# A new order list for a fused attention and token-mixing kernel, planned with other costs for the turned tiles of u

## Chip, cores and metric

The kernel runs on one core of one Trainium2 chip. The metric is the device time of one execution in microseconds (us), as the median of several runs; lower is better.

## What is computed

Two layers follow each other. The first is attention with 8 heads of 64 over 768 tokens, for 4 batches, where a token sees the 96 tokens up to itself and the first 8 tokens of all, with a bias that falls with the distance. The second takes its output as x (4 x 768 x 512) and mixes tokens and channels:

```
scores = q @ k.T / 8 + bias            # kept: 96 local columns and the 8 global ones
x      = softmax(scores) @ v           # heads side by side: 512 channels
theta  = x @ w_theta
y      = w_tok_r @ (x * cos(theta)) + w_tok_i @ (x * sin(theta))
u      = x + y
out    = u + relu(u @ w_ch)
```

## The kernel before

Tokens lie in 6 tiles of 128 (`NT`), heads in 4 pairs (`NP`). Each batch b goes through four stages, which are written down as about a thousand steps: `attention(b, p)` for each pair of heads, `theta(b)` for each tile of tokens, `mixing(b)` and `channel(b)`.

- `attention` turns q and k (on TensorE, L555, or for later batches on VectorE, L560, into `kq`), copies some keys aside (`kS`, L572 and L573), makes scores (TensorE, L611), exponents (ScalarE, L619), weighs them with the bias (VectorE, L628 and L633), multiplies with v (L678; some rows of v are copied to `vs` first, L439 and L443) and divides by the sums (VectorE, L698 and L699, into `x`). x is then turned on TensorE (L720) and copied to `xT` (L723).
- `theta` multiplies xT with w_theta (L796), takes cosine and sine on ScalarE (L804 and L807, into `cs`) and makes `zri` = x times both on VectorE (L813).
- `mixing` runs over two halves of the tokens and four chunks of channels. Each of these 8 sums takes 12 matmuls of 384 columns (L838), in groups of 4 that each wait for two tiles of `zri`, and ends with the addition of xT on VectorE (L847, into `uT`).
- `channel` multiplies uT with w_ch (L874), for each of 6 tiles of tokens, and needs u in its natural layout (`un`) for the last sum. In batches 0 and 3 TensorE turns it (L870). In batches 1 and 2 (`u_far`) the tile is turned by `turn_far`, described next. In these batches ScalarE makes the relu (L906) and GpSimd the sum (L909); elsewhere VectorE does both (L900). The result is stored from SyncE's queue (L917).

`turn_far` takes a tile out to DRAM and back. VectorE turns squares of 32 x 32 into one of two buffers (`squares_turn`, L756, shown as `w_nat<-uT` in the profile, since the buffers lie in `w_nat`'s place). SyncE issues four DMAs, one for each quarter of the partitions, that write the squares to DRAM at their turned places (`out_there`, L760, `far_u<-w_nat`), and then one that reads the tile back (`back`, L765, `un<-far_u`). As there are two buffers, the L756 of a tile waits until the DMAs of the tile two before have landed.

No loop fixes the order in which the engines get these steps. A planner (`Plan.order`) simulates the engines with a cost for each step and a delay (`HOP`) between a step and one on another engine that needs it, picks steps by priority, and issues them in the order of its planned starts. Two tables, keyed by the number of a step, move it: `plan.shifts` adds to its priority, `plan.only` fixes its engine where several could do it. On the chip each engine then works through its own queue in that order and waits wherever a semaphore is not there yet, so an instruction that waits holds up all that stands behind it in its queue. A step's cost has no effect on the chip but through this order. The steps of `turn_far` are, in the planner:

```
s1 = add("DVE", 0.12 + n * T / 960.0, squares_turn, ready + log[-2:-1] + s_wT[1], prio)
i1 = add("SP", 4 * 0.45, out_there, [s1], prio)
h1 = add("HW", 0.22 * n, lambda: None, [i1], 0)
log.append(h1)
i2 = add("SP", 0.45, back, [h1] + free, prio)
return add("HW", 0.1 * n, lambda: None, [i2], 0)
```

Here n is 4 for a tile of u, HW is a pretended engine for the time of the transfers, and `HOP["HW"]` is the delay after it.

Loads come from GpSimd's queue (`load`, with L392 and L477 for q and k, L397 for v); the 36 k and 36 q loads of L477 each fetch a block of 32 columns. GpSimd also does its share of the copies and the twelve sums L909, in the same queue.

Of the kernel before, what the change touches and what calls it, by code (L numbers as in the profile page):

```python
# [48 lines left out]
        self.end = None  # L49


HOP = {"PE": 0.28, "ACT": 0.18, "DVE": 0.18, "POOL": 0.25, "SP": 0.0, "DMA": 1.6, "STORE": 1.5, "LAND": 0.0, "HW": 2.0}

# [10 lines left out]
class Plan:  # L66
# [12 lines left out]
    def add(self, *a, **k):  # L79
        s = Step(*a, **k)  # L80
        self.steps.append(s)
        return s
# [141 lines left out]
def kernel(  # L224
# [15 lines left out]
    T = 128  # L240
    NT = S // T
    DM = H * D
    NP = H // 2
# [16 lines left out]
    def wide(bank):  # L260
        return PS[bank.got]

    def narrow(bank):
# [19 lines left out]
    x_t = [sb.tile([T, NP, NT, T], BF, name=f"x_{i}") for i in range(2)]  # L283
    xT = [sb.tile([T, NP, NT, T], BF, name=f"xT_{i}") for i in range(2)]
# [17 lines left out]
    r_t = [spare[:, (2 + 2 * i) * DM:(4 + 2 * i) * DM].bitcast(FP) for i in range(2)]  # L302
    plan = Plan(N_WIDE, N_NARROW)
    plan.shifts = {
        111: -90, 121: -459, 127: -298, 132: -268, 139: -9, 141: -38, 163: 504, 175: -9, 183: -174, 184: -602,
        194: 118, 196: 173, 199: -116, 204: -309, 205: -290, 208: 715, 215: 265, 219: 866, 221: 499, 223: 142,
        226: -289, 228: 607, 229: -721, 231: 76, 237: 504, 239: 1014, 244: 40, 247: -27, 248: -23, 251: -275,
        252: 324, 255: 54, 260: -47, 262: -53, 263: 789, 267: 222, 271: 1188, 275: 1795, 287: 280, 297: -209,
        298: 384, 304: 101, 305: 151, 310: -165, 312: -26, 336: -182, 372: 626, 391: -244, 408: -608, 412: 250,
        424: -45, 425: -223, 428: -44, 438: 124, 440: -117, 441: 1504, 444: 411, 448: 813, 452: -183, 457: -142,  # L310
        459: 5, 467: -339, 492: -90, 507: 231, 532: 229, 573: 345, 603: -266, 613: 117, 616: -5, 629: -91,
        632: -223, 635: 421, 638: -81, 647: -434, 649: 607, 653: 325, 655: -397, 656: -123, 665: -99, 668: 610,
        674: -2583, 675: 104, 677: -1014, 678: -634, 680: 199, 683: 347, 684: 205, 694: -193, 695: -59, 696: -155,
        698: -817, 704: 82, 708: 415, 714: 1451, 720: -238, 722: -196, 724: -915, 726: 411, 735: 115, 740: -165,
        765: 22, 851: 366, 880: -74, 893: 450, 900: -148, 903: -381, 904: 234, 910: 1872, 921: 605, 928: 2328,
        929: 2961, 946: -125, 950: 695, 952: -307, 956: -727, 980: 148, 994: 166, 1004: 1458, 1014: -220, 1015: -59,
        1020: 41, 1021: 512, 1028: -146, 1034: 53, 1035: 1834, 1043: 104, 1044: 100,
    }
    plan.only = {
        38: "POOL", 45: "POOL", 64: "POOL", 67: "POOL", 77: "POOL", 112: "DVE", 149: "DVE", 176: "POOL", 191: "ACT",  # L320
        194: "ACT", 228: "ACT", 244: "DVE", 281: "DVE", 287: "ACT", 299: "ACT", 318: "POOL", 333: "ACT", 337: "POOL",
        389: "ACT", 553: "DVE", 613: "DVE", 616: "DVE", 649: "DVE", 810: "POOL", 831: "DVE", 852: "DVE", 894: "POOL",
        951: "ACT",
    }
    add = plan.add
    ANY = list(range(N_WIDE + N_NARROW - 1, -1, -1))
# [209 lines left out]
    th_log, cs_log, o_log, mix_log, ch_log = {}, [], [], {}, {}  # L536

    def attention(b, p):
        pr = 1000 * b + 100 * p
        n = b * NP + p  # L540
# [4 lines left out]
        old = att_log.get(n - 3, [[], None])  # L545
# [38 lines left out]
        for g, (c0, n_c) in enumerate(groups):  # L584
# [50 lines left out]
            if by_pe:  # L635
                need.append(add("PE", 0.107 * n_c, far_off, [tk if (b, p) not in by_dve else None, old[1], s_dist, s_I[h0], s_I[h0 + 1]], pr + 18 + g,
                                takes=sc, dense=True, ins=4))
            s1 = add("PE", 0.0535 * n_c * cold, scores, need, pr + 20 + g, takes=None if by_pe else sc, tiled=1,
                     ins=8 if g == 0 else 16)
# [46 lines left out]
        for t0, t1 in ([(0, 2), (2, 4), (4, 6)] if fine else [(0, NT)]):  # L686
            nt = t1 - t0
            away = (b, p) in x_far
            mine = po[t0 // 2:t0 // 2 + 1] if fine else po

            def norm(t0=t0, t1=t1, nt=nt, mine=mine):
                dst = x_t[b % 2][:, p, t0:t1, :].rearrange("p t (h d) -> p h t d", h=2)
                if len(mine) == 1:
                    if fine:
                        ps = narrow(mine[0])[:, 0:2 * nt * (D + 1)].rearrange("p (h t d) -> p h t d", h=2, t=nt)
                    else:
                        ps = wide(mine[0])[:, :, 0:NT * (D + 1)].rearrange("p h (t d) -> p h t d", t=NT)
                    nc.vector.reciprocal(rc[:, :, t0:t1], ps[:, :, :, D])  # L698
                    nc.vector.tensor_mul(dst, ps[:, :, :, 0:D],  # L699
                                         rc[:, :, t0:t1, None].to_broadcast([T, 2, nt, D]))  # L700
                else:
                    for hh in range(2):
                        ps = narrow(mine[hh])[:, 0:NT * (D + 1)].rearrange("p (t d) -> p t d", t=NT)
                        nc.vector.reciprocal(rc[:, hh, :], ps[:, :, D])
                        nc.vector.tensor_mul(dst[:, hh, :, :], ps[:, :, 0:D],
                                             rc[:, hh, :, None].to_broadcast([T, NT, D]))
            nm = add("DVE", 0.55 if fine else 0.85 + 0.3 * len(po), norm,
                     [value_steps[t0 // 2] if fine else last] + [z_done[b - 2, st] for st in range(NT) if b >= 2],
                     pr + 60 + t0, frees=mine)
            if away:  # L710
                cx = turn_far(f"x{b}{p}", NT, x_t[b % 2][:, p, :, :], xT[b % 2][:, p, :, :], [nm], mix_log.get(b - 2, []), pr + 70)
                for t in range(t0, t1):
                    xT_done[b, p, t] = cx
                continue
            bk = Bank(False, ANY)

            def turn_x(t0=t0, t1=t1, bk=bk):
                ps = narrow(bk).bitcast(BF)
                for t in range(t0, t1):
                    nc.tensor.transpose(ps[:, (t - t0) * T:(t - t0 + 1) * T], x_t[b % 2][:, p, t, :], ident)  # L720

            def copy_x(copy, t0=t0, t1=t1, nt=nt, bk=bk):
                copy(out=xT[b % 2][:, p, t0:t1, :].rearrange("p t c -> p (t c)"),  # L723
                     in_=narrow(bk).bitcast(BF)[:, 0:nt * T])
            tx = add("PE", 0.0567 * nt, turn_x, [nm], pr + 70 + t0, takes=bk, ins=2 * nt)
            cx = any_of(copy_x, [tx] + mix_log.get(b - 2, []), pr + 71 + t0,
                        {"DVE": (0.08 + 0.07 * nt, 0.0), "ACT": (0.2 + 0.084 * nt, 0.0)}, frees=[bk])
            for t in range(t0, t1):
                xT_done[b, p, t] = cx
# [15 lines left out]
            got.append(any_of(cp, [t1], prio + st, {"DVE": (0.5, 0.0), "ACT": (0.72, 0.0)}, frees=[bk]))  # L745
        return got

    def turn_far(name, n, src, dst, ready, free, prio):


        log = sq_log[n]
        sq = sq_t[n][len(log) % 2]
        away = far_away.tile([n, T, T], BF, name=f"far_{name}")

        def squares_turn():
            nc.vector.transpose(out=sq[:, 0:n, :], in_=src)  # L756

        def out_there():
            for g in range(4):
                nc.sync.dma_start(  # L760
                    out=away.rearrange("n (j b) (i a) -> i b (n j) a", b=32, a=32)[g],
                    in_=sq[32 * g:32 * g + 32, 0:n, :].rearrange("b n (j a) -> b (n j) a", a=32))

        def back():
            nc.sync.dma_start(out=dst, in_=away.rearrange("n q a -> q n a"))  # L765
        s1 = add("DVE", 0.12 + n * T / 960.0, squares_turn, ready + log[-2:-1] + s_wT[1], prio)
        i1 = add("SP", 4 * 0.45, out_there, [s1], prio)
        h1 = add("HW", 0.22 * n, lambda: None, [i1], 0)
        log.append(h1)
        i2 = add("SP", 0.45, back, [h1] + free, prio)  # L770
        return add("HW", 0.1 * n, lambda: None, [i2], 0)

    sq_log = {NT: [], NP: []}
    s_wT = [None, None]
    sins = []
    by_two = ()
    z_done, u_done = {}, {}
# [77 lines left out]
    def channel(b):  # L855
        for tt in range(NT):
            pr = 1000 * (b + 1) + 500 + 10 * (NP * (tt // 3 + 1)) + 5 + tt
            late = b == B - 1 and tt >= parts[b][-1][0]
# [3 lines left out]
            o, un = o_t[n_o[0] % 4], un_t[n_o[0] % 4]  # L862
            n_o[0] += 1
            old = [o_log[-4]] if len(o_log) >= 4 else []
# [17 lines left out]
            away = (b, tt) in u_far  # L882
            if away:
                cu = turn_far(f"u{b}{tt}", NP, uT[b % 2][:, :, tt * T:(tt + 1) * T],
                              un.rearrange("p (c a) -> p c a", c=NP), u_done[b, tt], old, pr - 300)
            for c0, c1 in split:
                more = -30 * (c0 > 0)
                tu = tu if away else add("PE", 0.06 * (c1 - c0), lambda f=turn, a=c0, z=c1: f(a, z), [tu] + u_done[b, tt][c0:c1],
# [7 lines left out]
            for hf in range(halves):  # L896
# [5 lines left out]
                if (b, tt) in pool_add:  # L902
# [8 lines left out]
                    s1 = add("POOL", 1.3, add_u, [r1, cu] + old, pr - 400)  # L911
                    add_log.append(s1)
                else:
                    s1 = add("DVE", 0.1 + 0.55 / halves, f_o, [t1[hf], cu] + old, pr - 400 + hf, frees=[bks[hf]])
# [75 lines left out]
```

## Time and profile before

| what | us |
|---|---|
| median of 3 runs (172.05 to 172.56) | 172.32 |
| the profiled execution, its own time | 172.21 |
| its span, first to last instruction | 170.4 |
| TensorE busy | 156.4 (92%) |
| VectorE busy | 138.5 (81%) |
| ScalarE busy | 119.8 (70%) |
| GpSimd busy | 106.6 (63%) |
| mean granted TensorE clock | 0.996 |

The profiled execution took 1.8 us more than its span, before the first and after the last instruction. PE is TensorE, DVE VectorE, ACT ScalarE, POOL GpSimd and SP SyncE; SPq is SyncE's sequencer, which issues DMAs. A row of the timeline gives the start in the span, the length, the engine, the line of the kernel, the operation and the tiles (out<-in), and in brackets the idle time of the engine before it and what ended that.

### The profile page before, as it was taken

How to read it: one execution, taken by the hardware profiler on the slowest of the kernel's cores; microseconds unless marked ns; L12 is line 12 of the kernel's file. 1: busy time of each engine (PE TensorE's matmuls, PEld its weight loads, DVE VectorE, ACT ScalarE, POOL GpSimd, SP SyncE). 2: the span in 40 equal slices, each digit the busy share in tenths (PEclk: the TensorE clock that was granted, in tenths of full speed). 3: DMA queues.
4: the chain of work that ended last, by engine and by line, in shares of the span. 5: the costliest groups of instructions: out<-in, count | busy, mean ns of one | idle time of the engine just before them, and what ended most of it. 6: DMA issues, size and time to landing. Idle time of an engine off the chain costs nothing.

```text
span 170.4 us, 4571 instructions
## 1 busy us (share of the span) xinstructions
PE 156.4 (92%) x1817; PEld 93.7 (55%) x1830; DVE 138.5 (81%) x260; ACT 119.8 (70%) x191; POOL 106.6 (63%) x140
## 2 busy tenths in 40 slices
PE   7867888999999999999999999489999999999990
PEld 2335564665675655556666654245566655556560
DVE  4687986868999999999999989989998877432662
ACT  6996898939999399999785387867736968600130
POOL 7997931338997999999999985844800502530000
PEclk9999999999999999999999999999999999999998
DMA  4999999999999999999999999957424466730135
GB/s 108 168 157 174 204 204 205 206 172 157 53 132 121 106 219 115 91 238 125 85 106 104 125 138 118 94 164 188 143 30 72 62 155 104 196 137 0 42 141 186
DMA packets 124549, 22.78 MB, mean 134 GB/s; under 512 B 113648, under 2 KB 121584, under 8 KB 124528
## 3 DMA queue, kind: packets, MB, share of 16 engines
q0 software_dynamic: 88976, 12.66, 107.5%
q1 hardware_dynamic: 35408, 9.70, 25.4%
q8 instruction: 14, 0.23, 0.6%
q10 hardware_dynamic: 144, 0.13, 0.2%
q14 instruction: 7, 0.06, 0.1%
HBM read 27.26 MB, written 7.86 MB: 206 GB/s over the span
## 4 chain that ended last, share of the span: by engine, by line
PE 63%; DMA 14%; POOL 7%; SPq 4%; DVE 4%; ACT 4%; issue 2%; DVEq 0%; POOLq 0%
PE ps L838 29%; PE ps L874 10%; DMA zri<-in_moe_w_tok_r_dram 9%; PE ps L796 8%; DMA far_u<-w_nat 6%; PE ps L611 5%; SPq L760 4%; PE ps L678 4%; POOL v L397 3%; PE ps L720 2%; PE ps L739 2%; POOL q L392 2%; PE ps L870 2%; POOL k L392 1%; ACT ex L619 1%
## 5 line engine op out<-in xcount | busy, mean ns | idle before, releaser
L838 PE MATMUL ps<-wT,zri 128*128 128x384 bf16 x384 | 70.0, 326 | 2.6 <-DVE zri L813 2.6
L838 PEld LDWEIGHTS <-zri 128*128 128x128 bf16 x384 | 34.9, 98 | 24.9 <-DVE zri L813 3.2
L619 ACT ACTIVATE ex<-ps 128x1024 bf16<-128x1024 f32 (+1 forms) x44 | 40.6, 949 | 7.9 <-PE ps L611 7.3
L909 POOL TENSOR_TENSOR o<-w_nat,un 128x512 f32<-128x512 f32 x12 | 15.3, 1287 | 25.7 <-issue 9.3
L477 POOL DMA_DIRECT2D k<-in_k_dram x36 | 26.1, 787 | 5.6 <-DMA w_nat<-in_moe_w_tok_i_dram 1.8
L477 POOL DMA_DIRECT2D q<-in_q_dram x36 | 26.2, 797 | 3.0 <-DMA v<-in_v_dram 1.9
L847 DVE TENSOR_TENSOR uT<-xT,ps 128x384 bf16<-128x384 bf16 x32 | 17.4, 547 | 8.0 <-PE ps L838 7.6
L874 PE MATMUL ps<-w_ch,uT 128*128 128x512 bf16 (+1 forms) x93 | 22.9, 370 | 0.5
L796 PE MATMUL ps<-w_th,xT 128*128 128x512 bf16 x90 | 22.7, 379 | 0.3
L813 DVE TENSOR_TENSOR zri<-x,cs 128x1024 bf16<-128x1024 bf16 x24 | 20.1, 858 | 3.0 <-ACT cs L807 2.8
L633 DVE TENSOR_TENSOR ex<-ex,Wm 128x1024 bf16<-128x1024 bf16 x28 | 19.4, 701 | 0.1
L397 POOL DMA_DIRECT2D v<-in_v_dram x16 | 17.7, 1104 | 1.8 <-DMA w_nat<-in_moe_w_tok_i_dram 1.8
L804 ACT ACTIVATE cs<-ps,halfpi 128x512 bf16<-128x512 f32 x24 | 16.2, 694 | 2.3 <-DVE zri L813 1.1
L699 DVE TENSOR_TENSOR x<-ps,rec 128x256 bf16<-128x256 f32 (+1 forms) x26 | 16.9, 650 | 0.9
L678 PEld LDWEIGHTS <-ex 128*128 128x128 bf16 x352 | 13.9, 97 | 5.3 <-issue 1.4
L678 PE MATMUL ps<-v,ex 128*128 128x65 bf16 x224 | 15.0, 193 | 1.0 <-ACT ex L619 1.0
L611 PE MATMUL ps<-kq 64*128 64x128 bf16 (+1 forms) x192 | 14.3, 226 | 0.6 <-DVE kq L560 0.3
L807 ACT ACTIVATE cs<-ps 128x512 bf16<-128x512 f32 x24 | 14.4, 605 | 0.5 <-PE ps L796 0.5
L879 ACT COPY un<-ps 128x512 bf16<-128x512 bf16 x7 | 4.0, 590 | 14.9 <-PE ps L870 14.9
L796 PEld LDWEIGHTS <-xT 128*128 128x128 bf16 x96 | 9.1, 98 | 9.4
L874 PEld LDWEIGHTS <-uT 128*128 128x128 bf16 x100 | 9.0, 97 | 7.9 <-issue 0.4
L723 ACT COPY xT<-ps 128x768 bf16<-128x768 bf16 (+1 forms) x14 | 8.3, 590 | 7.1 <-PE ps L720 7.1
(78 smaller groups left out, 236.0 us busy)
## 6 DMA issues: line engine op xcount, KB each, us to landing
out_dram<-o SPq DMA_DIRECT2D x23, 256.0 KB, 2.8
v<-in_v_dram POOLq DMA_DIRECT2D x16, 192.0 KB, 6.0
k<-in_k_dram POOLq DMA_DIRECT2D x36, 48.0 KB, 4.7
q<-in_q_dram POOLq DMA_DIRECT2D x36, 48.0 KB, 4.5
far_u<-w_nat SPq DMA_DIRECT2D x48, 32.0 KB, 2.7
un<-far_u SPq DMA_DIRECT2D x12, 128.0 KB, 2.8
zri<-in_moe_w_tok_r_dram POOLq DMA_DIRECT2D x2, 576.0 KB, 13.0
w_nat<-in_moe_w_tok_i_dram POOLq DMA_DIRECT2D x2, 576.0 KB, 17.1
```

Of the source, the lines that this page charges most:

```text
L397: nc.gpsimd.dma_start(out=v_t[b % 2][:, h0:h0 + n, :, 0:D].rearrange("p h t d -> p (h t) d"), in_=v[b, h0:h0 + n].rearrange("h (t p) d -> ...
L477: nc.gpsimd.dma_start(out=squares(dst, b, h0).rearrange("p (j c) -> p j c", c=32)[r0:r0 + 32], in_=src[b, h0 + hh, :, 32 * dh:32 * dh + 32 ...
L611: nc.tensor.matmul(ps[hh][:, col * T:(col + w) * T], lhsT=lhsT, rhs=kq3[R, i // 3, 1, i % 3 * T:(i % 3 + w) * T], start=not by_pe, stop=no ...
L619: nc.scalar.activation(dst, wide(sc[0])[:, :, 0:n_c * T], AF.Exp, scale=scale)
L633: nc.vector.tensor_mul(dst, dst, w)
L678: nc.tensor.matmul(dst, lhsT=l, rhs=r, start=(i == 0), stop=(i == len(mms) - 1))
L699: nc.vector.tensor_mul(dst, ps[:, :, :, 0:D], rc[:, :, t0:t1, None].to_broadcast([T, 2, nt, D]))
L796: nc.tensor.matmul(tiles()[:, i, :], lhsT=xT[b % 2][:, p, st + i, :], rhs=w_th[:, p, :], start=(p == 0), stop=(p == NP - 1))
L813: nc.vector.tensor_mul(zri[b % 2][:, st, :, :].rearrange("p w (c d) -> p w c d", c=NP), x_t[b % 2][:, None, :, st, :].to_broadcast([T, 2, ...
L838: nc.tensor.matmul(narrow(bk)[:, 0:nt * T], lhsT=zri[b % 2][:, st, wi, c * T:(c + 1) * T], rhs=wT[wi][:, st, cols], start=(k + i == 0), st ...
L847: nc.vector.tensor_add(uT[b % 2][:, c, cols], xT[b % 2][:, c, n0:n0 + nt, :].rearrange("p t c -> p (t c)"), narrow(bk)[:, 0:nt * T])
L874: nc.tensor.matmul(narrow(bks[hf])[:, 0:wide_n], lhsT=uT[b % 2][:, c, tt * T:(tt + 1) * T], rhs=w_ch[:, c, hf * wide_n:(hf + 1) * wide_n], ...
```

## The change

The costs of a tile that is turned through DRAM are changed in the planner, with another number for batch 1 (2.5) than for batch 2 (0.3), and both tables are made anew for them. No computation, tile, buffer or DMA is added or removed.

```diff
-HOP = {..., "LAND": 0.0, "HW": 2.0}
+HOP = {..., "LAND": 0.0, "HW": 1.4}
...
     plan.shifts = {
-        111: -90, 121: -459, 127: -298, 132: -268, 139: -9, ...
+        26: 675, 67: 708, 97: 6, 111: -163, 127: 1472, ...
     }
     plan.only = {
-        38: "POOL", 45: "POOL", 64: "POOL", 67: "POOL", 77: "POOL", ...
+        67: "DVE", 76: "ACT", 112: "DVE", 130: "DVE", 131: "DVE", ...
     }
...
-    def turn_far(name, n, src, dst, ready, free, prio):
+    def turn_far(name, n, src, dst, ready, free, prio, late):
...
-        s1 = add("DVE", 0.12 + n * T / 960.0, squares_turn, ready + log[-2:-1] + s_wT[1], prio)
-        i1 = add("SP", 4 * 0.45, out_there, [s1], prio)
-        h1 = add("HW", 0.22 * n, lambda: None, [i1], 0)
+        s1 = add("DVE", 0.17 + n * T / 960.0, squares_turn, ready + log[-2:-1] + s_wT[1], prio)
+        i1 = add("SP", 2.0 + 0.2 * late, out_there, [s1], prio)
+        h1 = add("HW", 0.1 * n, lambda: None, [i1], 0)
         log.append(h1)
         i2 = add("SP", 0.45, back, [h1] + free, prio)
-        return add("HW", 0.1 * n, lambda: None, [i2], 0)
+        i2.ways["SP"] = (0.45, back, late)
+        h2 = add("HW", 0.1 * n, lambda: None, [i2], 0)
+        h2.ways["HW"] = (0.1 * n, h2.emit, late)
+        return h2
...
                 cu = turn_far(f"u{b}{tt}", NP, uT[b % 2][:, :, tt * T:(tt + 1) * T],
-                              un.rearrange("p (c a) -> p c a", c=NP), u_done[b, tt], old, pr - 300)
+                              un.rearrange("p (c a) -> p c a", c=NP), u_done[b, tt], old, pr - 300, 2.5 if b == 1 else 0.3)
```

The third number of an entry in `ways` is a delay before the step may start. The tables have 155 entries before and 147 after; no shift is the same in both, and 5 of the fixed engines are. In the changed file the lines of `turn_far` are one lower (L755, L759 and L764) and those of `theta` and all below it two higher (L815 for `zri`, L840 for the mixing, L911 for GpSimd's sums).

## Prediction

> **What bounds the kernel now.** First the page. TensorE is busy for 92% of the span, and its slices fall short in two places: up to 28 us, and at 106 to 119 us. GpSimd is full up to 106, mostly with loads.
>
> ```profile
> PE   7867888999999999999999999489999999999990
> POOL 7997931338997999999999985844800502530000
> ```
>
> Between the two TensorE never waits for 0.15 us at a time, so the kernel is its work plus these idle times. The order adds or removes no matmul, so what it can move is the idle time: 5.2 us up to 28 us (the bracketed waits of PE's timeline, the start included) and 2.9 us at 106 to 117. PE's timeline shows the second place:
>
> ```profile
> 105.80 1.14 PE L838 MATMUL ps<-wT,zri 128*128 128x384 bf16 x6
> 109.03 0.50 PE L838 MATMUL ps<-wT,zri 128*128 128x384 bf16 x2 [2.10 <-DVE zri L813]
> ...
> 111.41 2.77 PE L838 MATMUL ps<-wT,zri 128*128 128x384 bf16 x16 [0.52 <-DVE zri L813]
> ...
> 116.83 0.34 PE L611 MATMUL ps<-kq 64*128 64x256 bf16 x4 [0.26 <-DVE kq L560]
> ```
>
> Each of the three waits for VectorE: 2.10 + 0.52 + 0.26 = 2.88 us. VectorE's own timeline, and GpSimd's beside it:
>
> ```profile
> 102.37 0.71 DVE L756 STREAM_TRANSPOSE w_nat<-uT 128x512 bf16<-128x512 bf16 x1 [0.89 <-DMA far_u<-w_nat]
> 103.01 0.65 DVE L813 TENSOR_TENSOR zri<-x,cs 128x1024 bf16<-128x1024 bf16 x1
> 103.58 0.70 DVE L756 STREAM_TRANSPOSE w_nat<-uT 128x512 bf16<-128x512 bf16 x1
> 104.20 4.78 DVE L813 TENSOR_TENSOR zri<-x,cs 128x1024 bf16<-128x1024 bf16 x3
> ...
> 112.95 0.71 DVE L756 STREAM_TRANSPOSE w_nat<-uT 128x512 bf16<-128x512 bf16 x1 [0.42 <-DMA far_u<-w_nat]
> ```
> ```profile
> 106.14 2.28 POOL L909 TENSOR_TENSOR o<-w_nat,un 128x512 f32<-128x512 f32 x2
> 108.35 1.09 POOL L443 COPY vs<-v 32x520 bf16<-32x520 bf16 x1
> ```
>
> Two things hold VectorE up. A turn L756 waits for a way out to land (0.89 and 0.42). And three zri take 4.78, where one takes 0.65: the third stretches to 108.98 while GpSimd makes two sums. Last, the DMAs, in the window 86 to 112 and then 124 to 150, with the median from issue to landing:
>
> ```profile
> far_u<-w_nat SPq DMA_DIRECT2D x20, 32.0 KB, 5.0
> ...
> un<-far_u SPq DMA_DIRECT2D x3, 128.0 KB, 6.0
> ```
> ```profile
> far_u<-w_nat SPq DMA_DIRECT2D x24, 32.0 KB, 2.2
> un<-far_u SPq DMA_DIRECT2D x6, 128.0 KB, 2.7
> ```
>
> Batch 1's tiles leave beside GpSimd's loads, and take twice as long. The change's premise is in the trace.
>
> **What the planner now reckons.** From the end of a turn to the release of its buffer it reckoned 1.8 + 0.88 + 2.0 = 4.7 us; now, for batch 1, 2.5 + 0.4 + 1.4 = 4.3. From there to the tile's return it reckoned 0.45 + 0.4 + 2.0 = 2.9; now 2.5 + 0.45 + 2.5 + 0.4 + 1.4 = 7.3. So the way back is longer, as the trace asks, but what VectorE's next turns wait for is the way out, and that is reckoned shorter. In the trace the ways out of batch 1 took, from first issue to last landing, 5.2 (86.25 to 91.49), 6.6 (90.33 to 96.96) and 7.8 us (94.42 to 102.25). Two tiles turned one right after the other, at 102.37 and 103.58, had their eighth quarter landed at 112.82: the chain has 0.32 us for the first issue at 103.11, and a last issue with its landing at 108.71 for 4.11, together 9.7 us.
>
> **The head, up to 28 us.** GpSimd's rows up to the weights' loads are the same in both orders, so the second half of w_tok_r lands as before (at 27.4, the chain's 14.49 us from 12.89), and TensorE waits for it 0.69. Ahead of that wait the new order has 4 theta matmuls more (0.86 us) and 8 value matmuls fewer (0.24), so up to 0.6 less is idle there. Other waits before it are reshuffled (far_off's matmuls stand earlier and wait for banks); I bound the place by -0.6 and +0.4 and take -0.2.
>
> **The first pair of turns.** In the new order TensorE has 164 mixing matmuls ahead of the first turn where it had 148, 22 more for values and 4 more for scores: 16 x 0.163 + 22 x 0.030 + 4 x 0.04 = 3.4 us. The first turn moves from 85.5 to 88.9. The second follows it behind one small copy, at 89.8: the new order has at the front the pair that the old one had at 102. SyncE then has eight quarters in a row, the first at 89.6.
>
> **The third turn** uses the second tile's buffer. Between stand 13 VectorE rows: a kq turn 0.97, three weighings 0.56 + 0.68 + 0.68, three norms 1.19 + 0.59 + 0.59, an xT copy 0.29 and two uT sums 1.10, which is 6.65, less 0.08 of overlap each, 5.6. TensorE sets the last of them: ahead of its values stand 24 mixing matmuls (3.9), 36 for values (1.1), 20 for scores (0.8), 14 turns of x (0.8), 4 of the channel stage (0.9) and two switches (0.2), 7.7 us after those of the first turn, so 96.6; with the norm VectorE is there at 97.2. By the old pair's 9.7 the eighth quarter lands at 99.3; by the 6.6 of single tiles at 96.2. The loads run here as they did there (GpSimd's L477 and L397 follow each other as before), so I take 98.9, near the pair: VectorE stands for 1.7. Behind it wait the norm of x, and for this TensorE's next turn of x (L720): with another 1.8 us of matmuls ahead of it TensorE comes there at 98.4, and gets x at 98.9 + 0.7 + 0.6 = 100.2. Idle on TensorE: 1.8, bounds 0 and 2.2. Before, nothing was idle here.
>
> **The fifth turn** needs the third's way out, from 99.6. With the fourth turn 1.7 us behind the third, the nearest row is the pair's first tile, 103.11 to 110.05: 6.9, so 106.5; bounds 5.2 and 7.8. VectorE's rows up to it (the fourth turn, a copy, a kq turn, two zri) take it to 104.0. It stands for 2.5, and behind it stand the zri that mixing waits for. VectorE stood 0.89 here before, and its zri 3.6. I take 1.8 us on TensorE, bounds 0.8 and 2.4.
>
> **The sixth turn** needs the fourth's way out, from about 101.9; the pair's second tile had 8.5 (104.28 to 112.82), so 110.4, where VectorE arrives at 109.7. TensorE: 0.5, bounds 0 and 1.2.
>
> **Switches.** TensorE goes into the scores' tiles of 64 rows and out once more than before (36 times for 35). A score after a mixing matmul starts 0.26 us after it instead of 0.16, and the matmul after a score 0.15 instead of 0.05: 0.2.
>
> **The rest.** After 117 TensorE has no wait over 0.1 us but one of 0.2. The new order has batch 2's turns in more even places, and its ways are 2.2 us: nothing, bounds -0.2 and +0.9 (a rival). The end of both orders is the same split sum and store.
>
> **Sum.** New idle 1.8 + 1.8 + 0.5 = 4.1, old 2.88: +1.2. Switches +0.2, head -0.2: +1.2. The rows used are all near the long end; taking 1.0, 172.21 becomes 173.2, and since the median stands 0.1 above the profiled execution, 173.3.
>
> **A rule weighed.** Of the three zri above the first two took 0.6 us each, so the third began at 105.4, and took 3.6 us; the two sums ran 106.14 to 108.42. The Trainium skill (SBUF — State Buffer, "Who interferes with whom") says that a Vector instruction with two SBUF inputs and a GpSimd instruction that reads SBUF block each other, and whichever issues first keeps the shared port for its whole length. The trace agrees at 142.99, where two zri took 2.03 beside a sum at 142.50. It does not explain the 0.7 us before 106.14, in which GpSimd issued a load. By that rule the old 2.10 is the price of two sums in a row and not of ways out, and it speaks for the new order, as the first rival.
>
> **Rival 1, faster.** Zri and GpSimd's sums block each other; the new order puts a vs copy and a pair of kS copies between the first and the second sum, so no zri can lose more than one sum, 1.16. If besides the eight quarters land within 7.6 us of 89.6 (from there the third turn is free), the sum is 172.3 - 2.62 (both zri waits) + 1.2 (one sum) + 0.2 - 0.3 = 170.8. For it: 5.2 and 6.6 of single tiles. Against: the only pair took 9.7. Chance 0.18.
>
> **Rival 2, no change.** The third turn's idle hides, and the fifth's and sixth's take the place of the old waits: 1.8 + 0.5 - 2.88 + 0.2 = -0.4, with the bounds of the fifth 171.9 to 172.8. For it: it needs only the third way in 7.6. Against: the row. Chance 0.17. A difference below 0.3% (0.5 us) is about what a measurement of this kernel cannot tell from none.
>
> **Rival 3, slower still.** On SyncE the ways back of the third and fourth tile now stand behind the issues of the fifth and sixth, which wait for VectorE. So un comes late, GpSimd's sums wait, and behind two of them stand the kS copies for the next scores. With one kS pair late by a sum (1.16 less 0.3) and the long bounds, 1.0 + 0.9 + 0.6 more: 174.8. For it: GpSimd stood 2.60 and 2.04 before two of its sums. Against: the first kS copies stand ahead of the second sum. Chance 0.13. This leaves 0.52 for the forecast, whose own range is 172.6 to 174.2.
>
> **Right or wrong.** Right: the first two turns at 88 to 90 one behind the other, then a third L755 with 1 to 2.5 us of idle from far_u, a PE row of L719 at 99 to 101 with 1 to 2.2 of idle, and another L840 wait for zri at 106 to 109. Wrong: PE without a gap over 0.3 up to 105, or the eighth quarter landed before 97.2. If the zri of 3.6 is gone and nothing stands in its place, rival 1 has it.

## The result and the profile after

| | before | changed |
|---|---|---|
| median | 172.44 (4 runs, 172.05 to 173.67) | 177.94 (4 runs, 176.79 to 181.13) |
| profiled execution | 172.21 | 176.79 |
| its span | 170.4 | 175.0 |
| TensorE's last matmul ends at | 166.6 | 171.2 |

The changed kernel takes 1.027 times as long, 95% interval 1.020 to 1.034. Forecast were 173.3, with a range of its own of 172.6 to 174.2, and 174.8 for the slowest rival: the direction is right, the size is far off. Ratios in this document leave out runs more than 1.5% above the fastest of their kernel, in which the chip was in a slower state. Medians are over all runs. The kernel before ran again beside each group of experiments, at medians of 172.9 to 174.4, and each ratio is to the runs beside it.

The page of the changed kernel, with the same rows as before and the granted clock:

```profile
PE   7867999999999999999999589985999989999991
POOL 7997924349989997999999954671430503520000
PEclk9999999999999999999999969999999999999998
```

A slice is 4.4 us. The dip at 106 to 119 is now two dips, at 97 to 101 and at 118, and next to the first the clock falls for one slice. PE's timeline at these places:

```profile
97.68 1.03 PE L798 MATMUL ps<-w_th,xT 128*128 128x512 bf16 x4
101.50 0.28 PE L719 MATMUL ps<-ident,x 128*128 128x128 bf16 x2 [2.79 <-DVE x L698]
101.69 1.57 PE L798 MATMUL ps<-w_th,xT 128*128 128x512 bf16 x4
...
116.15 2.11 PE L840 MATMUL ps<-wT,zri 128*128 128x384 bf16 x12 [0.67 <-DVE uT L849]
120.15 0.23 PE L610 MATMUL ps<-kq,kS 64*128 64x128 bf16 x2 [1.89 <-DVE kq L559]
```

The 2.10 and 0.52 for `zri` are gone. In their place TensorE waits 2.79 for x, and then runs four theta matmuls in 1.57 that took 1.03 just before: this is the half clock, granted from 102.0 to 105.4. Later it waits 1.89 for `kq`. VectorE's rows say why, and below them GpSimd's:

```profile
100.20 0.71 DVE L755 STREAM_TRANSPOSE w_nat<-uT 128x512 bf16<-128x512 bf16 x1 [3.31 <-DMA far_u<-w_nat]
...
107.05 0.71 DVE L755 STREAM_TRANSPOSE w_nat<-uT 128x512 bf16<-128x512 bf16 x1 [0.46 <-DMA far_u<-w_nat]
...
110.67 0.71 DVE L755 STREAM_TRANSPOSE w_nat<-uT 128x512 bf16<-128x512 bf16 x1 [0.87 <-DMA far_u<-w_nat]
...
116.03 2.97 DVE L627 TENSOR_TENSOR ex<-ex,Wm 128x768 bf16<-128x768 bf16 x1
```
```profile
115.75 0.61 POOL L442 COPY vs<-v 32x520 bf16<-32x520 bf16 x1
116.33 2.26 POOL L911 TENSOR_TENSOR o<-w_nat,un 128x512 f32<-128x512 f32 x2
```

The third turn stands 3.31 for a way out. And a weighing that takes 0.50 elsewhere takes 2.97: it began beside GpSimd's copy of v, and two sums in a row followed that copy. The `kq` that TensorE waits for stands behind the weighing. The DMAs of the window 86 to 112 are no slower than before (5.0 and 6.0 there):

```profile
far_u<-w_nat SPq DMA_DIRECT2D x22, 32.0 KB, 4.4
...
un<-far_u SPq DMA_DIRECT2D x3, 128.0 KB, 4.6
```

To add up, I took from each stretch of TensorE's timeline the time that its matmuls need at full clock by the paces of the prediction (0.163 for one of mixing, and so on). What is left is called TensorE's excess below, in us:

| stretch | before | changed | difference | forecast |
|---|---|---|---|---|
| 0 to 28 | 7.25 | 6.24 | -1.0 | -0.2 |
| 28 to 60 | 0.14 | 0.83 | +0.7 | 0 |
| 60 to 97 | 0.18 | 0.21 | 0 | +0.2 |
| 97 to 101.8 | 0 | 3.04 | +3.0 | +1.8 |
| 101.8 to 125 | 3.27 | 4.36 | +1.1 | -0.6 |
| 125 to the end | 0.46 | 1.13 | +0.7 | 0 |
| sum | 11.3 | 15.8 | +4.5 | +1.2 |

The spans of the two profiled executions differ by 4.6, so the table holds nearly all of that. How it falls to the stretches depends on the paces taken, by some 0.3 (an estimate, from doing it again with other paces for the scores). The profiled execution of the changed kernel is the fastest of its four; the medians differ by 5.5, and for the other 0.9 there is no profile.

### The profile page after: what moved, and what is told of

The parts are those of the page before. It is cut to its first block, busy times and chain, and to the rows that moved or that the text cites. A ratio compares the mean times of both kernels' runs of the same rounds, so it can differ in the third digit from the quotient of the medians.

```text
span 175.0 us, 4571 instructions
## 1 busy us (share of the span) xinstructions
PE 159.0 (91%) x1817; PEld 93.8 (54%) x1830; DVE 138.5 (79%) x262; ACT 120.6 (69%) x190; POOL 105.9 (61%) x139
## 4 chain that ended last, share of the span: by engine, by line
PE 47%; DMA 23%; POOL 11%; DVE 10%; SPq 5%; issue 2%; DVEq 0%; POOLq 0%
PE ps L840 25%; DMA k<-in_k_dram 11%; PE ps L876 6%; DMA far_u<-w_nat 6%; PE ps L798 5%; DMA v<-in_v_dram 4%; PE ps L610 4%; SPq L759 4%; POOL k L476 3%; DVE kq L559 3%; POOL v L396 3%; PE ps L677 2%; DMA q<-in_q_dram 2%; DVE ex L627 2%; POOL q L391 2%
## 5 line engine op out<-in xcount | busy, mean ns | idle before, releaser
L840 PE MATMUL ps<-wT,zri 128*128 128x384 bf16 x384 | 70.8, 326 | 0.7 <-DVE uT L849 0.7
L840 PEld LDWEIGHTS <-zri 128*128 128x128 bf16 x384 | 34.9, 98 | 23.8 <-issue 1.7
L911 POOL TENSOR_TENSOR o<-w_nat,un 128x512 f32<-128x512 f32 x12 | 15.2, 1270 | 22.5 <-DMA un<-far_u 11.5
L476 POOL DMA_DIRECT2D q<-in_q_dram x36 | 25.5, 714 | 4.4 <-DMA k<-in_k_dram 1.9
L876 PE MATMUL ps<-w_ch,uT 128*128 128x512 bf16 (+1 forms) x93 | 24.4, 381 | 0.3
L798 PE MATMUL ps<-w_th,xT 128*128 128x512 bf16 x90 | 23.6, 390 | 0.3
L806 ACT ACTIVATE cs<-ps,halfpi 128x512 bf16<-128x512 f32 x24 | 17.0, 707 | 8.3 <-PE ps L798 8.3
L632 DVE TENSOR_TENSOR ex<-ex,Wm 128x1024 bf16<-128x1024 bf16 x28 | 20.3, 740 | 0.7 <-ACT ex L618 0.7
L815 DVE TENSOR_TENSOR zri<-x,cs 128x1024 bf16<-128x1024 bf16 x24 | 17.2, 736 | 2.7 <-ACT cs L809 2.6
L396 POOL DMA_DIRECT2D v<-in_v_dram x16 | 17.0, 1063 | 1.5 <-DMA w_nat<-in_moe_w_tok_i_dram 1.5
L881 ACT COPY un<-ps 128x512 bf16<-128x512 bf16 x9 | 5.1, 592 | 15.5 <-PE ps L872 15.5
L755 DVE STREAM_TRANSPOSE w_nat<-uT 128x512 bf16<-128x512 bf16 x12 | 8.4, 705 | 6.5 <-DMA far_u<-w_nat 6.4
```

The source lines that it names most:

```text
L396: nc.gpsimd.dma_start(out=v_t[b % 2][:, h0:h0 + n, :, 0:D].rearrange("p h t d -> p (h t) d"), in_=v[b, h0:h0 + n].rearrange("h (t p) d -> ...
L476: nc.gpsimd.dma_start(out=squares(dst, b, h0).rearrange("p (j c) -> p j c", c=32)[r0:r0 + 32], in_=src[b, h0 + hh, :, 32 * dh:32 * dh + 32 ...
L632: nc.vector.tensor_mul(dst, dst, w)
L798: nc.tensor.matmul(tiles()[:, i, :], lhsT=xT[b % 2][:, p, st + i, :], rhs=w_th[:, p, :], start=(p == 0), stop=(p == NP - 1))
L806: nc.scalar.activation(cs[:, 0, 0:per, :], tiles(), AF.Sin, bias=halfpi)
L815: nc.vector.tensor_mul(zri[b % 2][:, st, :, :].rearrange("p w (c d) -> p w c d", c=NP), x_t[b % 2][:, None, :, st, :].to_broadcast([T, 2, ...
```

## Experiments on the changed kernel

**Four buffers.** The turned squares get four buffers in place of two, in room that lay free; the order stays as it is.

```diff
-    sq_t = {NP: [spare[:, i * DM:(i + 1) * DM].rearrange("p (n a) -> p n a", a=T) for i in range(2)]}
+    sq_t = {NP: [spare[:, i * DM:(i + 1) * DM].rearrange("p (n a) -> p n a", a=T) for i in (0, 1, 6, 7)]}
...
-        sq = sq_t[n][len(log) % 2]
+        sq = sq_t[n][len(log) % 4]
```

> The changed kernel with four buffers for the turned squares instead of two, and the same order of all instructions. Theory A (the third turn on VectorE waits for the second tile's way out, TensorE stands 2.8 us behind it, and that standing makes the granted clock fall to 0.5 for 3.4 us): no wait of L755 for far_u at 97 to 100, no gap over 0.5 us on TensorE before 105, granted clock 1.0 throughout, and 3.0 + 1.7 us less: about 172.5 us. Rival B (the clock falls for a reason of its own): the gap is gone, but a stretch of clock 0.5 stays, about 174. Rival C (what waits next, zri or loads, is late anyway): the gap moves by a microsecond or two and stays, 175 to 177.

Measured: 174.58, ratio to before 1.013 (1.006 to 1.020). The wait at 98.7, the half clock behind it and the held weighing are all gone. The third turn and the weighing on VectorE are now:

```profile
100.60 0.70 DVE L755 STREAM_TRANSPOSE w_nat<-uT 128x512 bf16<-128x512 bf16 x1
...
115.57 0.71 DVE L627 TENSOR_TENSOR ex<-ex,Wm 128x768 bf16<-128x768 bf16 x1
```

One wait of 1.14 is left on TensorE between 96 and 122, behind a copy of v for which VectorE stood 2.01. From 28 us on TensorE's excess is 3.0, less than the 4.1 of the kernel before. But its profile lost 4.0 in the head, where two waits near each other (1.16 and 1.74, the second for a load of k) were followed by half clock for ten us. So two buffers and a late way out are the cause of the loss that begins at 97. That the weighing got through is also a matter of time: it ended at 116.28, and the first of the two sums now began at 116.63.

**The clock held up.** Twelve matmuls on zeros stand in the wait of the third turn.

```diff
             def turn_x(t0=t0, t1=t1, bk=bk):
+                if (b, p, t0) == (2, NP - 1, 4):
+                    for _ in range(12):
+                        nc.tensor.matmul(narrow(bk), lhsT=nought[:, 0:T], rhs=nought, start=True, stop=True)
                 ps = narrow(bk).bitcast(BF)
                 for t in range(t0, t1):
```

> The changed kernel with 12 matmuls of 512 columns (2.6 us, their results overwritten) ahead of the turn of x that TensorE stands 2.79 us for. All waits stay. Theory A: TensorE is not idle there, so the clock stays at 1.0: 1.7 us less, about 175.1 us, with the x norm still late (DVE idle 3.3 before the third turn). Rival B (the clock's fall has nothing to do with the idle time): clock 0.5 for 3.4 us as before, 176.8 or more.

Measured: 177.49, ratio 1.029 (1.023 to 1.035), no less than without. The clock was 1.0 throughout, and PE's timeline (lines from L719 on are three higher there) shows what the half clock had covered:

```profile
98.61 2.75 PE L719 MATMUL ps<-nought 128*128 128x512 bf16 x12
...
108.58 0.82 PE L843 MATMUL ps<-wT,zri 128*128 128x384 bf16 x4 [1.80 <-DVE zri L818]
...
113.60 0.50 PE L843 MATMUL ps<-wT,zri 128*128 128x384 bf16 x2 [1.12 <-DVE zri L818]
...
120.85 0.23 PE L610 MATMUL ps<-kq,kS 64*128 64x128 bf16 x2 [1.85 <-DVE kq L559]
```

The first two are the forecast's waits of the fifth and sixth turn (1.8 and 0.5): these turns stood 2.19 and 1.70 for `far_u`, with the `zri` behind them. With a slower TensorE the waits vanish, since it comes later to a VectorE that is late anyway. So the half clock costs nothing here that the times show.

**The third turn moved**, with its way out (steps 472 and 473), behind the norm, the xT copy and the addition that it had held up.

```diff
     order = plan.order()
+    place = {id(s): i for i, s in enumerate(plan.steps)}
+    for what, behind in ((472, 447), (473, 472)):
+        one = plan.steps[what]
+        order.remove(one)
+        order.insert(next(i for i, s in enumerate(order) if place[id(s)] == behind) + 1, one)
```

> The changed kernel with the third turn of batch 1 (and its way out) moved behind the norm of x, the xT copy and the uT sum that stood behind it in VectorE's queue. The two buffers stay. Theory A: the norm runs at 96.9, TensorE's turn of x does not wait, the third turn still waits until about 100 but with less behind it: TensorE's idle at 98.7 falls from 2.8 to under 1.0, the clock stays at 1.0, 173 to 174 us. Rival C (the xT copies and the fourth turn behind it matter as much): idle of 1.5 to 2.5 a little later, 175 to 176.5.

Measured: 177.62, ratio 1.018 (1.009 to 1.028), which rests on the two runs of 174.94 and 176.79; the profile is of another, of 178.45. Its waits have moved, not gone: 1.49 at 100.9, 2.38 for `zri` at 106.0, 1.90 for `kq` at 117.9. A gain of the move isn't clear of the noise, since the interval takes in the 1.027 of the changed kernel.

**Two sums left out.** GpSimd's sums of tiles 2 and 3 of batch 1, the two of 116.33, are not made (these tiles of the output are not computed).

```diff
-                    def add_u(o=o, r_o=r_o, un=un):
-                        nc.gpsimd.tensor_add(o, r_o, un)
+                    def add_u(o=o, r_o=r_o, un=un, tt=tt):
+                        if (b, tt) not in ((1, 2), (1, 3)):
+                            nc.gpsimd.tensor_add(o, r_o, un)
```

> The changed kernel without the two sums of GpSimd for tiles 2 and 3 of batch 1, the ones at 116.3 and 117.4; their tiles of the result are not computed. Theory D (these two sums hold VectorE's weighing of 2.97 us at 116.0, and through it the kq turn and TensorE's 1.89 us at 118.3): the weighing takes 0.55, the 1.89 us gap falls below 0.3, and 1.6 to 1.9 us less: about 175 us. Rival E (the weighing waits for something else, such as its exponents or GpSimd's copy): it stays near 3 us and the time stays within 0.5 of the changed kernel's.

Measured: 176.45, ratio 1.021 (1.015 to 1.027). The weighing is short:

```profile
117.33 0.70 DVE L627 TENSOR_TENSOR ex<-ex,Wm 128x768 bf16<-128x768 bf16 x1
```

The 1.89 is gone, and 0.97 for `uT` at 116.5 is all that TensorE waits there. So the sums did hold the weighing. The time fell by less than the 1.6 to 1.9 expected; in this profile TensorE's wait for x was 3.67, longer than the 2.79. The price of the two sums is 1.1 us by the ratios (1.027 and 1.021) and 1.7 by TensorE's excess between 112 and 125 (2.70 and 1.04).

**Another queue.** The way out of the second tile leaves from ScalarE's queue.

```diff
-                nc.sync.dma_start(
+                (nc.scalar if name == "u10" else nc.sync).dma_start(
...
```

The rest of the edit places that step behind the exponents of 90.0.

> The changed kernel, with the four DMAs that take the second turned tile of batch 1 out issued from ScalarE's queue, behind its exponents at 90.0, and not from SyncE's behind the first tile's four. Theory Q (SyncE's queue: eight quarters in a row, each issue waiting for earlier ones): the eighth quarter lands at 95.5 to 97.5 and not at 100.1, VectorE's wait before the third turn falls from 3.31 to under 1.0, TensorE's 2.79 at 98.7 to under 0.7, time -1.5 to -3 against the changed kernel. Rival D (the DMA engines, shared with GpSimd's loads): the eighth quarter still lands at 98.5 to 100.5, TensorE's wait stays over 1.8, time within 0.8 of the changed kernel.

Measured: 177.87, ratio 1.028 (1.019 to 1.037). This run was 1.6 us late when its ways out began: first issue 91.27, eighth landing 100.25, so 9.0 us for the eight quarters where it had been 10.4. Those on ScalarE's queue took longer each:

```profile
far_u<-w_nat SPq DMA_DIRECT2D x4, 32.0 KB, 4.2
far_u<-w_nat ACTq DMA_DIRECT2D x4, 32.0 KB, 5.8
```

And ScalarE stood while it issued them, so that scores waited for its exponents:

```profile
92.40 2.35 ACTq L759 DMA_DIRECT2D far_u<-w_nat  x4
```
```profile
96.36 0.23 PE L610 MATMUL ps<-kq,kS 64*128 64x128 bf16 x2 [1.85 <-ACT ex L618]
```

Theory Q accounts for 1.4 of the 2.6 to 4.6 us it promised. The third turn ran without a wait, but only since VectorE itself came later, behind ScalarE. The greater part is left to the DMA engines, which GpSimd's loads kept busy (rival D); that is argued, since no run took the loads away.

**The head filled**, on top of four buffers, with six matmuls on zeros ahead of the turning of the last pair of batch 0.

```diff
         def turn():
+            if (b, p) == (0, 3):
+                for _ in range(6):
+                    nc.tensor.matmul(narrow(bank[0]), lhsT=nought[:, 0:T], rhs=nought, start=True, stop=True)
```

> The changed kernel with four buffers, as in the first experiment, and six more matmuls of 512 columns on zeros (6 x 0.216 = 1.3 us) ahead of the turning of the last pair's k and q of batch 0, where TensorE waited 1.74 for a load at 12.8. Theory H (the head's clock): in the first experiment TensorE's excess over its bare work up to 28 us was 10.2 against 6.2 in the changed kernel, because two idle times of 1.16 and 1.74 us close together halved the clock from 14 to 24 us; with the gap filled the clock stays at 1.0 there, the head ends like the changed kernel's, and the time is 170.5 to 172.5, at or below the kernel before. Rival L (the late load alone): the clock costs nothing, since the head ends with the landing of w_tok_r; the time stays at 174 to 175.

Measured: 175.08 beside 174.36 of the kernel before. The ratio, 0.996 (0.986 to 1.007), rests on two of ten runs, of 171.73 and 173.65. The head of the profile kept its clock at 1.0, with waits like the changed kernel's (1.16, 0.57 and shorter), as theory H has it. TensorE waited 2.47 at 111.9, since VectorE's copy of v stood for the last load:

```profile
113.55 0.30 DVE L438 COPY vs<-v 128x520 bf16<-128x520 bf16 x1 [1.32 <-DMA v<-in_v_dram]
```

**That copy moved** behind the addition and the weighing after it.

```diff
     order = plan.order()
+    place = {id(s): i for i, s in enumerate(plan.steps)}
+    one = plan.steps[872]
+    order.remove(one)
+    order.insert(next(i for i, s in enumerate(order) if place[id(s)] == 897) + 1, one)
```

> The changed kernel with four buffers, the six matmuls in the head, and one VectorE copy of v (vs) that waited 1.32 for the last load of v moved behind the addition into uT and the weighing that stood after it. Theory W (what is left of the new order's loss once the buffers are four is that copy, at the head of VectorE's queue): TensorE's wait of 2.47 at 112 falls to 0.5 to 1.0, no half clock behind it, time 1.5 to 2.5 below the version without the move, 0.5 to 2 below the kernel before. Rival F (the tiles' ways and the loads only push the wait on): another wait of 1.5 or more on TensorE between 112 and 120, time within 0.8 of the version without the move and of the kernel before.

Measured: 173.98 beside 173.61, ratio 0.996 (0.991 to 1.001): no faster than before (rival F). The 2.47 went, and 1.44 stood at 115.8, for a relu that had waited for a buffer of GpSimd's sum. In this profile the clock fell in the head all the same, so the six matmuls don't hold it for sure.

**The changed kernel again**, unaltered.

> The changed kernel again, on this chip beside the others. Theory: its two idle times have causes that do not depend on the run: VectorE's third turn waits 2.5 to 3.5 for far_u, TensorE 2 to 3 behind it at 98 to 100, and a weighing beside two GpSimd sums in a row takes over 2.5 and leaves TensorE 1.5 to 2 at 117 to 119; time 2 to 3.5% above before. Rival (chance in the landings): one of the two is under 1.0 this time, and the time is within 1.5% of before.

Measured: 178.50, ratio 1.030 (1.024 to 1.035). The eight quarters took 11.3 (90.18 to 101.44), and VectorE's rows behind the two waits of the first profile are there again:

```profile
101.56 0.71 DVE L755 STREAM_TRANSPOSE w_nat<-uT 128x512 bf16<-128x512 bf16 x1 [4.16 <-DMA far_u<-w_nat]
...
118.29 1.82 DVE L627 TENSOR_TENSOR ex<-ex,Wm 128x768 bf16<-128x768 bf16 x1
```

TensorE stood 3.64 behind the first, and 1.69 before `kq`. The first is longer than expected, the weighing shorter (over 2.5 was expected), and neither wait is the accident of one profile.

## Experiments on the kernel before

**Four buffers**, the same edit.

> The kernel before, its order as it was, with four buffers for the turned squares in place of two, so that none of its turns waits for the way out of the tile two before. Theory A (the 2.10 us at 106.9 are the shared port: the third zri held up by two GpSimd sums in a row): VectorE's waits of 0.89 and 0.42 for far_u go, the zri beside the sums still takes over 3 us, TensorE's waits of 2.10 + 0.52 + 0.26 = 2.9 fall by no more than VectorE's 0.9 + 0.4 = 1.3, time -0.3 to -1.3 against before. Rival B (the ways out are what holds VectorE): the 2.10 falls below 0.5, time -2 to -2.9.

Measured: 173.54 beside 174.36, ratio 1.003 (0.997 to 1.009). No turn waits now, and yet the three `zri` take longer than the 4.78 of before:

```profile
104.06 5.27 DVE L813 TENSOR_TENSOR zri<-x,cs 128x1024 bf16<-128x1024 bf16 x3
```

TensorE still waits 1.00 + 0.52 + 0.52. Theory A has it: the sums bound this place. The 0.3 to 1.3 us that it allowed the ways out can't be told from the noise: the medians are 0.8 apart, the ratio shows no gain.

**No sums beside the zri.** Those of tiles 0 and 1 of batch 1 are not made.

```diff
-                    def add_u(o=o, r_o=r_o, un=un):
-                        nc.gpsimd.tensor_add(o, r_o, un)
+                    def add_u(o=o, r_o=r_o, un=un, tt=tt):
+                        if (b, tt) not in ((1, 0), (1, 1)):
+                            nc.gpsimd.tensor_add(o, r_o, un)
```

> The kernel before without GpSimd's sums of tiles 0 and 1 of batch 1 (those two tiles of the output are not computed; the stores still go). Theory A (shared port): the third zri falls from 3.6 to 0.6 or 0.7 us, TensorE's waits of 2.10 and 0.52 fall to under 0.6 together, time -1.5 to -2.5 against before. Some of it could be that GpSimd's vs copy behind the sums comes 2.2 us earlier; then a VectorE row other than zri moves. Rival B (ways out): the zri is still late, at least 1.5 of the 2.6 stays, time 0 to -0.8.

Measured: 172.23 beside 174.36, ratio 0.990 (0.974 to 1.006). The `zri` are short, but the next way out takes over, and less than the 1.5 to 2.5 expected can be shown:

```profile
105.44 1.85 DVE L813 TENSOR_TENSOR zri<-x,cs 128x1024 bf16<-128x1024 bf16 x3
...
113.69 0.71 DVE L756 STREAM_TRANSPOSE w_nat<-uT 128x512 bf16<-128x512 bf16 x1 [2.84 <-DMA far_u<-w_nat]
```

TensorE waits 2.06 behind that turn. With either cause taken away alone, the other holds TensorE up.

**Both at once**: four buffers for the squares and four for the relu, and the two sums, with their stores, moved behind GpSimd's kS copy.

```diff
...
-                    r_o = r_t[len(add_log) % 2]
+                    r_o = r_t[len(add_log) % 4]
...
+    for what, behind in ((469, 894), (459, 469), (470, 459), (460, 470)):
+        one = plan.steps[what]
+        order.remove(one)
+        order.insert(next(i for i, s in enumerate(order) if place[id(s)] == behind) + 1, one)
```

> The kernel before with four buffers for the squares and four for the relu, and GpSimd's sums of tiles 0 and 1 of batch 1 (with their stores) moved behind its kS copy, so that no sum runs beside the zri and no turn waits for a way out. Theory A with the ways out (in the kernel before each of the two hides the other: four buffers alone left 2.0 of TensorE's 2.9, no sums alone left a wait of 2.1 for uT): now both go, the zri take 0.6 to 0.7 each, TensorE waits under 1.0 in all between 100 and 118, time -1.5 to -2.5 against before. Rival M (the sums, moved, hold other VectorE rows with two SBUF inputs, and un's buffers come free later): a weighing or zri beside the moved sums takes over 2 us, TensorE waits 1.5 or more, time 0 to -0.8.

Measured: thirteen runs in two groups, 168.1 to 170.5 and 172.1 to 175.6. The ratio of 0.977 (0.971 to 0.983) is that of the lower group; the median of all, 172.08, is 0.991 of the 173.61 beside it. The profile fell in the upper group, and shows what held that run up:

```profile
106.41 5.61 DVE L814 TENSOR_TENSOR zri<-x,cs 128x1024 bf16<-128x1024 bf16 x2
```
```profile
108.10 2.26 POOL L910 TENSOR_TENSOR o<-w_nat,un 128x512 f32<-128x512 f32 x2
110.33 1.14 POOL L910 TENSOR_TENSOR o<-more,un 128x512 f32<-128x512 f32 x1
```

The second of these `zri` began at 107.45, and three sums in a row held it until 112.03. TensorE waited 3.31 behind it. That the lower group's `zri` escaped the sums is inferred; there is no profile of that group.

**The sums far behind.** They stand behind the other four of the batch, again with four buffers for the squares, with six for o and un, and the relu goes straight into o.

```diff
...
-                    r_o = r_t[len(add_log) % 2]
+                    r_o = o
...
+    for what, behind in ((469, 509), (459, 469), (470, 510), (460, 470)):
+        one = plan.steps[what]
+        order.remove(one)
+        order.insert(next(i for i, s in enumerate(order) if place[id(s)] == behind) + 1, one)
```

> The kernel before with four buffers for the squares, six for o and un, the relu written straight into o, and GpSimd's sums of tiles 0 and 1 of batch 1 (with their stores) moved behind the other four sums of the batch, where they can't run beside the zri even if these come late. Theory A with the ways out: in the profile of the version before this one the last zri took 4.57 because three sums in a row ran from 108.10 to 111.47, and its runs lay in two groups (168.1 to 170.5, and 172.1 to 175.6) by whether the zri met the sums; now the group above is gone, the zri take 0.6 to 1.2 each, TensorE waits under 1.2 in all between 100 and 118, time 2 to 3 below the kernel before. Rival M: six sums nearly in a row from 114 on hold weighings (2 us or more each) between 114 and 124, TensorE waits there for VectorE 1.5 or more, time 0 to -1.

Measured: 170.06 (169.18 to 171.49) beside 173.51, ratio 0.986 (0.979 to 0.993): faster than both kernels. PE's and the clock's slices:

```profile
PE   7778979999999999999999999999999999999990
...
PEclk9998799999999999999999999999999999999999
```
```profile
106.41 1.60 DVE L813 TENSOR_TENSOR zri<-x,cs 128x1024 bf16<-128x1024 bf16 x2
```

Between 24 and 123 us TensorE has no wait over 0.3. The ways out took a median of 4.9 in this window, as long as ever; no turn waits for them. What the added buffers for o and un give by themselves was not tried apart.

## Why the prediction was wrong

**Head.** Forecast -0.2. Measured -1.0 up to 28 us and +0.7 from there to 60: -0.3. The second half of w_tok_r did not land as before but at 26.4, and TensorE had no wait for it. The second part was not foreseen; PE shows two waits of 0.2 in it, and the rest stays open. (The old kernel's bracketed waits up to 28 us add up to 6.0, not to the 5.2 that the prediction read; nothing else hangs on it.)

**First pair.** Forecast 88.9 and 89.8, first issue 89.6. Measured 88.92, 89.73, 89.66.

**Third turn, the first step that failed.** The place, the chain and the row of TensorE were right, and VectorE was there at 96.9 for the forecast's 97.2. Mis-sized was the way out: I took 9.3 us from first issue to eighth landing, between 6.6 and the old pair's 9.7, and held 9.7 to be the long end. It took 10.4, and 11.3 in the repetition. VectorE so stood 3.31 for 1.7, and TensorE 2.79 (3.64 in the repetition) for 1.8, with a bound of 2.2. The mistake is to have made the only row for a pair a bound: it was one draw. Nor was it like the new pair: GpSimd issued its last load at 105.11, in the midst of the old one, while in the new order it issues loads up to 103.83, beyond the pair's last landing. That these loads made the difference fits, but no run shows it apart.

**Fifth and sixth turn.** Forecast 1.8 and 0.5. In the changed kernel's profile they are not to be seen, with the clock held up they are 1.80 and 1.12. The sum lacked the half clock, but this took their place and added nothing.

**The weighed rule, the second step that failed.** I applied it to `zri` alone, and to the first two sums alone, and let it speak for the new order ("no zri can lose more than one sum, 1.16"). That was true of the `zri` (2.09 at 104.5, one sum). But the sums of tiles 2 and 3 came in a row at 116.33 and held a weighing, which reads two tiles of SBUF as `zri` does. The forecast put nothing there; TensorE waited 1.89, and 1.1 to 1.7 of it went when these sums were left out. The prediction said that after 117 there is nothing but the turns of batch 2; the order of GpSimd's later sums against VectorE's rows was never laid out. By the table this place came out 1.7 above the forecast, and that of the third turn 1.2; together they are most of the 3.3 by which the sum was short.

**Old waits and the rest.** The 2.88 fell away as forecast, though one `zri` still took 2.09. Batch 2 had one wait of 0.75 at 142.7, and the stretch from 125 on +0.7 in all, inside the bound of 0.9 for which I took 0. The switches' 0.2 can't be seen apart.

**The taken value.** The sum was +1.2, and I went down to 1.0 because the rows were "near the long end". The terms' own upper ends add up to 2.2 + 2.4 + 1.2 + 0.9 + 0.4 + 0.2 - 2.88 = +4.4, nearly the 4.6 measured between the profiled executions, while the slowest rival stopped at +2.5: I had not let several terms be long together, though the same loads run beside all the ways out. That +4.4 comes near is in part luck, since it has nothing for the held weighing.

**Rivals.** The first fell with the 10.4, and so did the second, whose sum has nothing for the third turn. (The second's 171.9 to 172.8 does not follow from the bounds of the fifth turn; with 0.8 and 2.4 it is 170.9 to 172.5.) The third had the right sign, but another mechanism: the first kS copy (109.36) waited for VectorE, not behind sums. Of the two things said to hold VectorE in the old kernel, the experiments on it show that the sums bound its place, and that the ways out stood right behind them.

## What to carry to other kernels

When two waits end on the same engine, take away each alone and both together before pricing either: here each hid the other, neither alone gave a gain clear of the noise (1.003 and 0.990), and both together, with more buffers for the sums, gave 1.4%. A rule on a shared resource is to be held against every instruction of that kind in the window, not just the one that showed it. And a planner with finer costs for transfers can still lose if it knows neither that two engines hold each other up nor how many buffers a run of tiles needs.

## What the runs showed of the hardware

**VectorE waits out a whole row of sums.** Held `zri` ended 0.56 after the last sum of an unbroken row, with one sum (106.03, 106.59), two (108.42, 108.98) and three (111.47, 112.03); a held weighing ended 0.41 after it (118.59, 119.00). In the repetition a pause of 0.12 between two sums was enough to let the weighing go after the first (it took 1.82 and not 2.97). The rule of the Trainium skill (SBUF — State Buffer, "Who interferes with whom") has the lock; that VectorE gets no turn between two sums in a row is this case's number. A copy ahead of the sums belongs to the row, as the one of 115.75 did. A copy of v right behind a sum let VectorE go first: it took 1.09 at 108.35, and 0.61 at 115.75.

**The hold begins before the sums.** The unexplained 0.7 of the prediction has a pattern: in the kernel before, in that with four buffers, in the changed one, and in this with the other queue or the moved turn, a `zri` that began 0.2 to 0.7 into GpSimd's issue of a load of v, right ahead of a sum, had all of its work still to do when the sum ended. The issue alone does not hold it: in the kernel before without the two sums a `zri` ran from 106.01 to 106.69, inside such an issue (105.73 to 106.75), and took 0.68. What holds it ahead of a sum stays open.

**Half clock after a window that is idle for little more than half.** The Trainium skill (TensorE: Matmul & The Clock Gate, "Part 1: The HAM clock gate") has the clock fall after an idle window of some 3.4 us, at a phase that the program doesn't set. Here it fell after idle times of 2.79 (from 102.0 to 105.4, one such window), 3.64 and even 1.90 (the moved turn), while 1.89, 2.10 and 2.38 (the moved turn again) left it alone. The phase fits that; that a whole window must be idle does not. In the traces the times between changes of the granted clock are multiples of 3.41 us (3.41, 6.83, 10.24, 95.57). Cut into windows in step with these changes, the traces between 90 and 165 us have a fall behind each window in which TensorE was idle for more than 0.54 of it (seven windows, the lowest at 0.543 with the other queue), and none behind the others (the highest at 0.541, with the clock held up). The wait of 2.38 lay across two windows, idle for 0.42 and 0.30. In the head, where matmuls are small, 0.43 was once enough.
